# Strassen's scheme for the last four chunks of the MLP's first product in blocks 0 and 1

## The chip, the cores and the metric

One Trainium2 chip, one core of it. The metric is the device time of one execution in microseconds. Engines in the text: TensorE (PE), VectorE (DVE), ScalarE (ACT), GpSimd (POOL), SyncE (SP, which issues most DMAs).

## The reference

Two layers, each a linear attention and an MLP, on 2048 tokens of width 448, all in fp32:

```
x = x + attention(layernorm(x))        # 16 heads of 28, feature map elu(t)+1
x = x + gelu(layernorm(x) @ w1 + b1) @ w2 + b2     # w1: 448 x 1792, w2: 1792 x 448
```

The same weights serve both layers.

## The kernel before, in words

The tokens are cut into 16 tiles of 128, and these into four blocks of 512 (tiles 0 to 3 are block 0, and so on). The hidden width of 1792 is cut into 14 chunks of 128. A value that takes part in a matmul is split into a high part, which the matmul keeps exactly, and a low part (the rest); a product is three matmuls, high by high, low by high and high by low. ACT makes the high part by a cast (`XH`, `gh`), DVE or POOL the low part by a subtraction (`XL`, `gl`).

`mlp1` is the first product of one chunk of one block, the classic way: 11 matmuls 128x512 into the bank `hp` (L1205), then gelu on ACT and the split of g. The 448 rows of w1 are three pieces of 128 and one of 64; the last piece's low terms share matmuls, hence 11. `mlp2` is the second product of the chunk: for each of the block's four tiles three matmuls 128x448 into the bank `y` (L1235 to L1237). After the last chunk DVE adds `y` to the residual in `r` (L1240, called evacuation here) and SP stores it. Four banks hold `y`, so a new block's second product can begin only as the old block's four tiles are evacuated.

Blocks 0 and 1 go through all 14 chunks this way (`classic`). Blocks 2 and 3 go together, two chunks at a time, by Strassen's scheme (`eight(l, k)`, k from 0 to 6): the tokens of the two blocks are the rows and the pair's two chunks are the columns of a 2x2 matrix product, which takes seven products instead of eight. A11 and A12 are the two halves of block 2's width, A21 and A22 those of block 3; S1 = A21 + A22, S2 = S1 - A11, S3 = A11 - A21, S4 = A12 - S2. The seven products are 6, 5, 5, 5, 6, 6 and 6 matmuls 128x512, 39 where the classic way has 44. They add up in the banks `hx`, `hy`, `hz` (L1147): product 1 begins `hx`, ACT keeps a copy of it as `s1`, and product 6 goes on in the same bank; DVE adds the parts to `s1`, `s2` and `s5`. Two of the four results (block 2's) go on to gelu, split and `mlp2`; block 3's are stored as g in `g_d` and read back as `gb` in a last stage (`rest`), which does block 3's second product.

The sums S and the splits of all seven A and S (`token_sum`, L1112, by POOL for the first half of a tile and DVE for the second; `token_piece`, L1117 and L1118) are made while block 1 is at its last chunks. The tiles come as `sp`: DVE transposes 32x32 squares (`turn`), and a store to DRAM and a load back bring them into place (`store_sq`, `spread`). The weights' pieces are made by a generator per pair of chunks, `chunks` for a classic pair and `sevens` for a Strassen pair, advanced one step at a time by `make(n)`; two pairs fit into `W1` at once.

Every engine runs its instructions in the order in which the program writes them. What other work stands where among the chunks of blocks 0 and 1 is set by the table `PLAN`: one entry for each chunk, and each token of an entry is a piece of work (`behind`): q and p are steps of the attention's second half, o its output product, n the layernorm of a token tile, sx and lx store and load of its squares, sS.. a token sum, tA.. and tS.. a split, r and b the residual's reload and the bias. `ORDER` does the same for the stage ahead of the MLP.

Of the kernel before, what the change touches and what calls it, by code (L numbers as in the profile page):

```python
# [22 lines left out]
def linear_attn_mlp_kernel(  # L23
# [278 lines left out]
    squares, stored, spreads = {}, {}, {}  # L302
# [22 lines left out]
    def spread(key, h):  # L325
        d = stored.pop((key, h))
        if key[0] == "m" and (key[2], h) == (2, 1):
# [382 lines left out]
    def stage_g(l, t, acc, mid=lambda: None):  # L710
# [86 lines left out]
    def phase1(l, tr):  # L797
        za = consts.tile([128, D], F32, name="za", tag="za")
        acc = []
        load_to(l, 4 if l == 0 else NORM[l][1][-1])  # L800
        if l == 0:
            launch(za)
            load_to(l, NORM[l][2][-1])
        for t in range(l == 0, NT):
            norm = NORM[l][t] if t < len(NORM[l]) else ()
            for tok in STEPS.get((l, t), STEP).split():
                if tok[1:].isdigit() and tok[0] in "anv":
                    {"a": stage_a, "n": stage_n, "v": stage_t}[tok[0]](l, int(tok[1:]))
                elif tok == "q1":
                    stage_qphi(1)  # L810
                elif tok == "sp":
                    for key, h in list(stored):
                        block(key)
                        spread(key, h)
# [100 lines left out]
    def trans_chunks(tr):  # L915
# [4 lines left out]
        def rows(src, out, at, lo, hi):  # L920
            r = lo
            while r < hi:
                n = min(hi, (r // G + 1) * G) - r
                act.dma_start(f(out[at + r - lo:at + r - lo + n]), f(src[r // G][r % G:r % G + n]))
                r += n

        for c in range(3):
            for src, k in ((tr.Mh, 0), (tr.Ml, 1)):
                rows(src, tr.ch[c][k], 0, c * 128, (c + 1) * 128)
                yield  # L930
        rows(tr.Mh, tr.cr, 0, TL, D)
        rows(tr.Ml, tr.cr, 64, TL, D)
        yield


# [136 lines left out]
    def m_prep(l, b, j):  # L1072
# [5 lines left out]
              {"A11": 0, "S1": 5, "S2": 4, "A12": 1, "S3": 6, "S4": 2, "A22": 3})  # L1078
    SUMS = {"S1": ("A21", "A22", OP.add), "S2": ("S1", "A11", OP.subtract),
# [5 lines left out]
    def all_of(l, k, name):  # L1085

        at = PLACES[k][name]
        if at < 4:
            return (XH, XL)[k][:, at * 1024:][:, :1024]
        if (l, k, name) not in tall:  # L1090
            tall[l, k, name] = wide(k, at - 4, name)
        return tall[l, k, name]

    def placed(l, k, name, h):
        return all_of(l, k, name).rearrange("p (c h n) -> p h c n", c=2, h=2)[:, h]
# [28 lines left out]
    class Pair:  # L1124


        def __init__(self, l, p, n):
            self.l, self.p, self.n = l, p, n
            self.g = {}

        def product(self, k):
            at, name = PRODUCTS[k]
            w = W1[:, self.n % 2]
            hi, lo = (all_of(self.l, k, name) for k in range(2))
# [19 lines left out]
        def gelu(self, x, f):  # L1154
            g = t512("e", 5, "g")
            i = 2 * self.p + 1 - f
            for h in range(2):
# [12 lines left out]
        def later(self, x, f):  # L1170
            g = self.gelu(x, f)
            i = 2 * self.p + f
            g_d[self.l, i] = dram([128, 512], F32, f"g_d{self.l}_{i}")
            sp.dma_start(g_d[self.l, i], g)
# [35 lines left out]
    def mlp2(l, b, i, then=lambda: None):  # L1210
        gh, gl = gs.pop(i)
        first, last = i == 0, i == NF - 1
        n = i ^ (b > 1)
        hi, lo = w2h[:, n], w2l[:, n]
        end = l == LAYERS - 1 and b == NB - 1
        if first:
            accs[l, b] = [bank("acc", 4, f"y{j}")[:, :D] for j in range(4)]
        acc = accs[l, b]
        for j in range(4):
# [18 lines left out]
            if stop:  # L1238
# [4 lines left out]
                if last:  # L1243
                    sp.dma_start(x_d[l + 1][t * 128:(t + 1) * 128, :], xs)

    accs = {}
# [7 lines left out]
        "p10 z11",  # L1254
        "p11 sq10 z12 ld20",
        "p12 z13 lq10 ld21",
        "p13 sq11 z20 g10 ld22",
        "q10 lq11 p20 z21 g11 ld23",
        "q11 o10 p21 sq20 z22 g12",
        "q12 n10 o11 p22 z23 g13 ld30",  # L1260
        "q13 n11 o12 sx10 ld31",
        "n12 o13 lq20 p23 sq21 z30 ld32",
        "n13 lx10 sx11 p30 z31 g20 ld33",
        "lq21 p31 z32",
        "lx11 q20 x10 x11 sq30 g21",
        "q21 x12 x13 o20 p32 z33 g22",
        "q22 n20 o21 lq30 g23",
        "q23 n21 o22 p33 sq31 sx20 g30",
        "q30 n22 o23 g31",
        "q31 lq31 n23 o30 sx21 g32",  # L1270
        "q32 n30 o31 g33 r10 r11",
        "q33 n31 o32 sx30 lx21 r12 r13",
        "n32 o33 lx20 tA111 b10",
        "n33 sx31 lx30 tA121 b11",
        "lx31 tA110 b12",
        "sS10 sS11 tA120 b13",
        "tS10 tS11 sS30 sS20",
        "sS40 tS20 sS31 sS21",
        "tS21 sS41",
        "tS40 tS41",  # L1280
        "tS30 tS31",
    )

    def behind(l, i, tr):
        for tok in sorted(PLAN[i].split(), key=lambda tok: tok[0] != "l"):
# [27 lines left out]
            elif name == "x":  # L1313
                m_part(l, k, j)
            elif name == "r":
# [5 lines left out]
    ahead = [(l, "x" if b == 2 else "c", p) for l in range(LAYERS) for b in range(3) for p in range(NP)]  # L1321

    def first_pair(l, b):
        return (l * 3 + b) * NP

    def classic(l, b, tr):

        if b == 0:
            mlp1(l, 0, 0)
            moves = trans_chunks(tr)  # L1330
        for i in range(NF):
            if i + 1 < NF:
                mlp1(l, b, i + 1)
            elif b == 0:
                mlp1(l, 1, 0)
            if b == 0:
                next(moves, None)
            n = first_pair(l, b) + i // 2 + 2
            late = b and i >= NF - 4
            if late:  # L1340
                make(first_pair(l, 2))
            elif i % 2:
                make(n)
            if i % 2 == 0 and (b == 0 or i < NF - 2):
                make(n + 1)
            behind(l, b * NF + i, tr)
            if b == 0 and 5 <= i < 9:
                add_bias(l, 0, i - 5)
            if b == 0 or i < NF - 2:
                mlp2(l, b, i)  # L1350
            if b == 0:
                next(moves, None)
            if late:
                make(first_pair(l, 2))
            elif i % 2 == 0:
                make(n)

# [22 lines left out]
    def eight(l, k):  # L1380

        n = first_pair(l, 2) + k
        c = Pair(l, k, n)
# [40 lines left out]
        else:  # L1424
            step()
            mlp2(l, 1, NF - 2)
            c.product(2)
            dve.tensor_tensor(s1, s1, c.Z, op=OP.add)
            token_piece(l, "A22", 0)
            c.high(s1, 0)  # L1430
            make(n + 2)
            step()
            c.product(5)
            s5 = c.keep(c.Y, "s5")
            step()
            c.product(6)
            s2 = c.keep(c.X, "s2")
            c.low(0)
# [6 lines left out]
            make(n)  # L1445
            step()
            c.product(3)
            dve.tensor_tensor(s2, s2, c.Y, op=OP.add)
            c.high(s2, 1)
# [9 lines left out]
    class Came:  # L1459
# [6 lines left out]
        def load(self, l, n=1):  # L1466
            for i in range(self.n, min(self.n + n, NF)):
                tag = "EEFFeeee"[i % 8]
                self.x[i] = t512(tag, 5 if tag == "e" else 2, "gb")
                sp.dma_start(self.x[i], g_d[l, i])  # L1470
# [69 lines left out]
    for l in range(LAYERS):  # L1540
# [11 lines left out]
        def ahead_pq(j):  # L1552
# [15 lines left out]
            sa=lambda j: spread(("m", l, 0), j), pl=ahead_pq, z=lambda j: q_z(l, j, 0, tr), pre=lambda j: make(first_pair(l, 0) + 2), b=biases)  # L1568
# [5 lines left out]
        for b in range(2):  # L1574
            classic(l, b, tr)
        for k in range(NP):
# [30 lines left out]
```

## Time and profile before

| | |
|---|---|
| three runs | 850.35 us median (849.75 to 850.36) |
| the profiled execution | 850.62 us, its span 848.9 us |
| granted TensorE clock | 0.999 |
| busy in the span | PE 842.9 us, DVE 574.2, ACT 510.4, POOL 386.4 |
| matmul groups | `hp` 392 and 224 on high and low tokens (L1205), `y` 447 at each of L1235 to L1237 |
| DMA | 142.92 MB, mean 168 GB/s |

The span is what the profile shows of the execution; the 1.72 us beside it lie around it. Busy times of engines overlap. A group's busy time is a sum of durations as recorded; recorded matmuls overlap their neighbours.

### The profile page before, as it was taken

To read this page: it belongs to the slowest core of one execution; us is meant where nothing else is said; L and a number is where in the kernel's file an instruction comes from. 1 tells how busy PE (TensorE), PEld (TensorE's weight loads), DVE (VectorE), ACT (ScalarE), POOL (GpSimd) and SP (SyncE) were. 2 spreads that over 40 slices of the span, in tenths; PEclk is the share of its full clock that TensorE was granted. 3 is DMA by queue.
4 is the path that set the end of the run, shared out by engine and by line. 5 is a ranking of instruction groups with operands and counts; after the bars stand their busy time and mean duration, and the time that the engine had idled before them with its cause. 6 is when DMAs were issued, how large, how long until landed. Compare 5 with 4: busy or idle time off the path is not lost.

```text
span 848.9 us, 12473 instructions
## 1 busy us (share of the span) xinstructions
PE 842.9 (99%) x4085; PEld 754.8 (89%) x4085; DVE 574.2 (68%) x1022; ACT 510.4 (60%) x1051; POOL 386.4 (46%) x460
## 2 busy tenths in 40 slices
PE   9999999999999999999999999999999999999998
PEld 8899988888888888889999998988888888888897
DVE  7899597768733765556788976868686358544443
ACT  7667666475777567564446665555667766656521
POOL 3456534555426754650532343145742367454320
PEclk9999999999999999999999999999999999999999
DMA  5365847767667034437645543477666641333261
GB/s 166 123 241 183 254 121 220 244 208 239 209 199 240 14 125 132 135 112 239 217 152 175 172 142 120 135 226 246 215 203 229 224 161 34 114 94 103 89 236 44
DMA packets 103637, 142.92 MB, mean 168 GB/s; under 512 B 9876, under 2 KB 90644, under 8 KB 103572
## 3 DMA queue, kind: packets, MB, share of 16 engines
q1 hardware_dynamic: 101156, 138.77, 50.1%
q10 hardware_dynamic: 2416, 3.36, 1.3%
q8 instruction: 32, 0.52, 0.3%
q14 instruction: 33, 0.27, 0.1%
HBM read 88.94 MB, written 49.02 MB: 163 GB/s over the span
## 4 chain that ended last, share of the span: by engine, by line
PE 96%; DVE 2%; DMA 1%; POOL 1%; issue 0%; ACT 0%; SPq 0%; DVEq 0%; POOLq 0%; ACTq 0%
PE hp L1205 16%; PE y L1236 11%; PE y L1235 11%; PE y L1237 10%; PE hx L1147 9%; PE G L724 7%; PE psk L382 7%; PE psq L382 7%; PE hy L1147 4%; PE hz L1147 2%; PE op L1022 2%; PE op L1021 2%; PE op L1023 2%; PE op L1011 1%; PE op L1010 1%; PE op L1012 1%
## 5 line engine op out<-in xcount | busy, mean ns | idle before, releaser
L1236 PE MATMUL y<-w2l,gh 128*128 128x448 f32 x447 | 164.1, 367 | 0.0
L1235 PE MATMUL y<-w2h,gh 128*128 128x448 f32 x447 | 162.3, 363 | 0.0
L1237 PE MATMUL y<-w2h,gl 128*128 128x448 f32 x447 | 160.8, 360 | 0.0
L1182 DVE TENSOR_TENSOR gl<-g,gh 128x512 fp32r<-128x512 f32 x84 | 70.1, 835 | 103.1 <-ACT gh L1178 103.0
L1205 PE MATMUL hp<-XH,W 128*128 128x512 f32 x392 | 123.3, 389 | 0.0
L1235 PEld LDWEIGHTS y<-w2h,gh 128*128 128x128 f32 x447 | 83.8, 187 | 9.3
L1236 PEld LDWEIGHTS y<-w2l,gh 128*128 128x128 f32 x447 | 83.9, 188 | 6.8
L1237 PEld LDWEIGHTS y<-w2h,gl 128*128 128x128 f32 x447 | 84.0, 188 | 5.4
L1205 PE MATMUL hp<-XL,W 128*128 128x512 f32 x224 | 85.2, 389 | 0.0
L1205 PEld LDWEIGHTS hp<-XH,W 128*128 128x128 f32 x392 | 73.5, 188 | 12.6
L1207 ACT ACTIVATE g<-hp,b1s 128x512 f32<-128x512 f32 x56 | 38.5, 688 | 60.8 <-PE hp L1205 58.2
L1038 POOL TENSOR_TENSOR brs<-bst,few 128x1 f32<-128x1 f32 x32 | 18.7, 585 | 118.2 <-ACT bst L1036 116.8
L1159 ACT ACTIVATE g<-s,b1s 128x256 f32<-128x256 f32 x84 | 38.2, 502 | 55.5 <-DVE s L1413 34.9
L382 PE MATMUL psk<-wk,XH 128*128 128x448 f32 x210 | 61.8, 364 | 0.0
L563 POOL TENSOR_TENSOR xnl<-x,xnh 128x384 fp32r<-128x384 f32 x32 | 35.4, 1106 | 55.6 <-ACT xnh L562 27.8
L382 PE MATMUL psq<-wq,XH 128*128 128x448 f32 x196 | 57.2, 366 | 0.3 <-DVE eq L401 0.3
L1178 ACT CAST gh<-g 128x512 fp32r<-128x512 f32 x84 | 52.2, 622 | 2.7
L425 POOL TENSOR_TENSOR W<-temp,W 128x256 fp32r<-128x256 f32 x56 | 48.2, 880 | 7.5 <-ACT W L424 7.5
L1205 PEld LDWEIGHTS hp<-XL,W 128*128 128x128 f32 x224 | 42.0, 188 | 8.8
L213 POOL TENSOR_TENSOR brs<-bve,few 128x1 f32<-128x1 f32 x31 | 17.1, 551 | 66.9 <-DVE bve L212 61.5
L724 PE MATMUL G<-kh,xnh 128*128 128x448 f32 x128 | 46.6, 367 | 0.0
L724 PE MATMUL G<-kl,xnh 128*128 128x448 f32 x128 | 46.1, 366 | 0.0
(252 smaller groups left out, 2107.5 us busy)
## 6 DMA issues: line engine op xcount, KB each, us to landing
temp<-in_B_w_dram SPq DMA_DIRECT2D x28, 384.0 KB
x<-in_A_x_dram SPq DMA_DIRECT2D x32, 224.0 KB
pq_d<-eq SPq DMA_DIRECT2D x32, 224.0 KB
pq<-pq_d SPq DMA_DIRECT2D x32, 224.0 KB
g_d<-g SPq DMA_DIRECT2D x28, 256.0 KB
x<-x_d SPq DMA_DIRECT2D x32, 224.0 KB
gb<-g_d SPq DMA_DIRECT2D x28, 256.0 KB
sq_a<-sq SPq DMA_DIRECT2D x13, 512.0 KB
```

What stands on the lines that cost most here:

```text
L382: pe.matmul(o, x, p, start=(i == 0), stop=(i == 10))
L425: pool.tensor_tensor(lo, x, f(hi), op=OP.subtract)
L724: pe.matmul(acc[c], w, k, start=first and c not in others[0], stop=last and c not in others[1])
L1147: pe.matmul(o, w, r, start=(k in (1, 5, 2) and i == 0), stop=(i == len(made) - 1), skip_group_check=True)
L1159: act.activation(g[:, s].rearrange("p (u i n) -> p i u n", u=2, i=4), x[:, s].rearrange("p (i u n) -> p i u n", u=2, i=4), AF.Gelu_apprx_t ...
L1178: act.copy(gh, g)
L1182: dve.tensor_sub(gl, g, f(gh))
L1205: pe.matmul(hp, w, r, start=(k == 0), stop=(k == len(made) - 1))
L1207: act.activation(g, hp, AF.Gelu_apprx_tanh, bias=b1s[:, i:i + 1])
L1235: pe.matmul(acc[j], gh[:, s], hi, start=first, stop=False)
L1236: pe.matmul(acc[j], gh[:, s], lo, start=False, stop=False)
L1237: pe.matmul(acc[j], gl[:, s], hi, start=False, stop=stop)
```

## The change

`CUT = 10`: the classic way now does chunks 0 to 9 of blocks 0 and 1. The new `joint(l, k)`, k = 0 and 1, does chunks 10 to 13 of both blocks by the same seven products, block 1 as A11 and A12 and block 0 as A21 and A22, so that block 1's own split tiles serve as two of the seven (`FRONT`). Block 1's g goes straight to its second product. Block 0's is stored to `g_d`, its second product of chunks 0 to 9 is evacuated early and stored as a partial sum (`part_d`), and a later pass (`remainder` and the first pair `eight(l, 0)`) does chunks 11, 10, 13 and 12 with g and the sum read back. Block 0's unsplit tiles are kept in SBUF for the sums. `PLAN` is new, with two places in an entry (ahead of the "|" and behind it); the sums and splits of blocks 2 and 3 now stand in the remainder and in `eight(l, 0)`. The pairs of chunks 10 to 13 get their weights by `sevens`. Of the seven copies of the attention's combined weights `wq` two go through SP's queue before the MLP and the other five through ACT's, three to a chunk in place of two; q_scale and q_z of the first tile of block 1 stand ahead of the MLP.

```diff
+    FRONT = {"S1": 0, "A22": 1, "A11": 2, "A12": 3, "S3": 4, "S4": 5, "S2": 6}
...
+    def front_piece(l, name, h):
+        x = front_view(l, name, h)
+        hi, lo = (front(l, k, name, h) for k in range(2))
+        act.copy(hi, x)
+        dve.tensor_tensor(lo, x, f(hi), op=OP.subtract)
...
-        first, last = i == 0, i == NF - 1
+        part = int(b == 0 and i >= CUT)
+        first, last = (i == LATER[0], i == LATER[-1]) if part else (i == 0, i == (NF if b else CUT) - 1)
...
+    def load_part(l, t):
+        xt[l, t] = t448("H", 8, f"r{l}_{t}")
+        sp.dma_start(xt[l, t], part_d[l, t])
...
     PLAN = (
...
-        "lx31 tA110 b12",
-        "sS10 sS11 tA120 b13",
-        "tS10 tS11 sS30 sS20",
...
+        "sS11 tA120 tA121 tS10 sS30 sS20 tA111 sS31 c12",
+        "tS11 sS21 tS20 tS21 sS40 sS41",
...
+    CUT = 10
+    LATER = (11, 10, 13, 12)
...
+    def joint(l, k, tr):
...
+        c.product(1)
+        s1 = c.keep(c.X, "s1")
...
+            c.product(6)
+            s2 = c.keep(c.X, "s2")
+            c.low(0)
+            behind(l, 26, tr)
+            mlp2(l, 1, CUT - 1)
+            step()
+            c.product(7)
+            dve.tensor_tensor(s5, c.X, s5, op=OP.add)
+            c.later(s5, 1)
...
+    def remainder(l, tr):
+
+        mlp2(l, 1, NF - 1)
+        for k in range(2):
+            divide(LATER[k + 1], came.pop(LATER[k + 1]))
+            behind(l, 24 + k, tr)
+            mlp2(l, 0, LATER[k])
...
     def eight(l, k):
...
-            step()
-            mlp2(l, 1, NF - 2)
+            mlp2(l, 0, LATER[2])
+            behind(l, 27, None)
             c.product(2)
+            make(n + 2)
+            divide(LATER[3], came.pop(LATER[3]))
             dve.tensor_tensor(s1, s1, c.Z, op=OP.add)
-            token_piece(l, "A22", 0)
-            c.high(s1, 0)
...
             c.product(5)
             s5 = c.keep(c.Y, "s5")
             c.product(6)
             s2 = c.keep(c.X, "s2")
+            c.high(s1, 0)
             c.low(0)
-            mlp2(l, 1, NF - 1)
+            make(n)
+            mlp2(l, 0, LATER[3])
...
             c.product(7)
             dve.tensor_tensor(s5, c.X, s5, op=OP.add)
+            for h in range(2):
+                token_piece(l, "A22", h)
             c.later(s5, 1)
-            token_piece(l, "A22", 1)
```

Three places in the first layer show how instructions move; the rows are an engine's instructions in its order, equal neighbours counted with x. The first is DVE in the first pair of blocks 2 and 3, from the addition to s1 to the first split of weights after the evacuations; before, the low parts of A22 (`XL<-sp,A_3357`) are apart, and r_4 to r_7 are block 1's residual:

```order
L1428 TENSOR_TENSOR s_3333<-s_3333,hz 128x512
L1118 TENSOR_TENSOR XL<-sp,A_3357 128x2x256
L457 COPY raw<-W_130 128x256
L1182 TENSOR_TENSOR gl<-g,gh 128x512
L1240 TENSOR_TENSOR r_4_2877<-y_2659,r_4_2877 128x448
...
L1240 TENSOR_TENSOR r_7_2951<-y_2662,r_7_2951 128x448
L1442 TENSOR_TENSOR s_3379<-hx,s_3379 128x512
L1118 TENSOR_TENSOR XL<-sp,A_3357 128x2x256
L479 TENSOR_TENSOR W_130<-raw,W_130 64x128
L466 TENSOR_TENSOR W_130<-raw,W_130 128x512
```

The same place of the changed kernel, where r_0 to r_3 are block 0's residual and L1594 and L1607 are the additions to s1 and s5:

```order
L1594 TENSOR_TENSOR s_3408<-s_3408,hz 128x512
L1229 TENSOR_TENSOR gl<-g,gh 128x512
L486 TENSOR_TENSOR W_130<-raw,W_130 64x128
L1288 TENSOR_TENSOR r_0_3236<-y_3358,r_0_3236 128x448
...
L1288 TENSOR_TENSOR r_3_3242<-y_3361,r_3_3242 128x448
L464 COPY raw<-W_130 128x256
L1607 TENSOR_TENSOR s_3452<-hx,s_3452 128x512
L1162 TENSOR_TENSOR XL<-sp,A_3506 128x2x256 x2
L1613 TENSOR_TENSOR s_3460<-s_3460,hy 128x512
L473 TENSOR_TENSOR W_130<-raw,W_130 128x512
```

Both low parts of A22 now stand together behind gl, the evacuations, the copy and the addition to s5.

The second place is DVE's making of sums and splits of blocks 2 and 3. Before, in the last chunks of block 1 (S_3146 and the `sp` written by L1112 are sums):

```order
L1112 TENSOR_TENSOR S_3146<-sp 128x2x256
L1118 TENSOR_TENSOR XL<-sp,A_3067 128x2x256
L1182 TENSOR_TENSOR gl<-g,gh 128x512
L1118 TENSOR_TENSOR S_3189<-S_3146,XH 128x2x256 x2
L1182 TENSOR_TENSOR gl<-g,gh 128x512
L1118 TENSOR_TENSOR S_3234<-sp,S_3233 128x2x256
L1112 TENSOR_TENSOR sp<-sp 128x2x4x64
L1112 TENSOR_TENSOR sp<-S_3146,sp 128x2x4x64
L457 COPY raw<-W_130 128x256
L1182 TENSOR_TENSOR gl<-g,gh 128x512
```

Changed, in the remainder and the first pair (`gl<-gb,gh` are the low parts of block 0's chunks that came back; the last is chunk 12's):

```order
L1162 TENSOR_TENSOR XL<-sp,A_3345 128x2x256 x2
L1162 TENSOR_TENSOR S_3350<-S_3288,XH 128x2x256
L1162 TENSOR_TENSOR XL<-sp,XH 128x2x256
L1156 TENSOR_TENSOR sp<-sp 128x2x4x64
L1229 TENSOR_TENSOR gl<-gb,gh 128x512
L1162 TENSOR_TENSOR S_3350<-S_3288,XH 128x2x256
L1156 TENSOR_TENSOR sp<-S_3288,sp 128x2x4x64
L1162 TENSOR_TENSOR S_3382<-sp,S_3381 128x2x256 x2
L1156 TENSOR_TENSOR sp<-sp 128x2x4x64
L1162 TENSOR_TENSOR S_3422<-sp,XH 128x2x256 x2
L1162 TENSOR_TENSOR XL<-sp,XH 128x2x256 x2
L1229 TENSOR_TENSOR gl<-gb,gh 128x512
```

The work that was spread over block 1's last chunks, each with a classic first product, now stands in one piece. The third place is TensorE at the start of the four last chunks of the two blocks, first of before (block 1's last chunk 13, then block 2 and 3's first product):

```order
L1205 MATMUL hp<-XH,W_130 128x512
L1205 MATMUL hp<-XL,W_130 128x512
L1147 MATMUL hx<-XH,W_130 128x512 x2
L1147 MATMUL hx<-XL,W_130 128x512
L1147 MATMUL hx<-XH,W_130 128x512 x2
L1147 MATMUL hx<-XL,W_130 128x512
L1235 MATMUL y_2659<-w2h,gh 128x448
```

Changed, the first joint pair, whose product 1 follows the output product of the last token tile (`op`):

```order
L1041 MATMUL op<-wq_1678,qh 128x448
L1042 MATMUL op<-wq_1678,ql 128x448
L1191 MATMUL hx<-XH,W_130 128x512 x2
L1191 MATMUL hx<-XL,W_130 128x512
L1191 MATMUL hx<-XH,W_130 128x512 x2
L1191 MATMUL hx<-XL,W_130 128x512
L1283 MATMUL y_2370<-w2h,gh 128x448
```

Where a classic product stood before, products of Strassen's scheme now stand in blocks 0 and 1 too.

More of the change, by code (lines that the diff above doesn't have):

```diff
@@ L325, in spread @@
     def spread(key, h):
-        d = stored.pop((key, h))
-        if key[0] == "m" and (key[2], h) == (2, 1):
+        d = stored[key, h]
+        if key[0] == "m" and key[2] == 0:
+            l = key[1]
+            if (l, h // 2) not in kept:
+                kept[l, h // 2] = wide(h // 2, 2, "sp", F32)
+            r = kept[l, h // 2][:, h % 2 * 512:][:, :512]
+        elif key[0] == "m" and key[2] == 1:
+            r = wide(h, 1, "sp", F32)
+        elif key[0] == "m" and (key[2], h) == (2, 1):
             r = wide(0, 2, "sp", F32)
@@ L913, in trans_ms, with trans_chunks, rows @@
         dve.tensor_sub(tr.Ml[g], tr.mp[g], f(tr.Mh[g]))
-    def trans_chunks(tr):
+    def trans_chunks(tr, queues=(sp, sp, act, act, act, act, act)):
         tr.ch = [(piece("q", c), piece("q", 3 + c)) for c in range(3)]
         tr.cr = piece("q", 6)
-        def rows(src, out, at, lo, hi):
+        queue = iter(queues)
+        def rows(src, out, at, lo, hi, eng):
             r = lo
@@ L928, in trans_chunks, with trans_on @@
             for src, k in ((tr.Mh, 0), (tr.Ml, 1)):
-                rows(src, tr.ch[c][k], 0, c * 128, (c + 1) * 128)
+                rows(src, tr.ch[c][k], 0, c * 128, (c + 1) * 128, next(queue))
                 yield
-        rows(tr.Mh, tr.cr, 0, TL, D)
-        rows(tr.Ml, tr.cr, 64, TL, D)
+        eng = next(queue)
+        rows(tr.Mh, tr.cr, 0, TL, D, eng)
+        rows(tr.Ml, tr.cr, 64, TL, D, eng)
         yield
+    def trans_on(tr, n):
+        if not hasattr(tr, "moves"):
+            tr.moves = trans_chunks(tr)
+        for _ in range(n):
+            next(tr.moves, None)
     pqt, qs, pzs = {}, {}, {}
@@ L1133, in product @@
             w = W1[:, self.n % 2]
-            hi, lo = (all_of(self.l, k, name) for k in range(2))
+            hi, lo = (all_of(self.l, self.b, k, name) for k in range(2))
             u = [w[:, i * 128:(i + 1) * 128] for i in at]
@@ L1216, in mlp2 @@
         if first:
-            accs[l, b] = [bank("acc", 4, f"y{j}")[:, :D] for j in range(4)]
-        acc = accs[l, b]
+            accs[l, b, part] = [bank("acc", 4, f"y{j}")[:, :D] for j in range(4)]
+        acc = accs[l, b, part]
         for j in range(4):
@@ L1243, in mlp2, with behind @@
                 if last:
-                    sp.dma_start(x_d[l + 1][t * 128:(t + 1) * 128, :], xs)
-    accs = {}
-    PLAN = (
[L1254 to L1274, printed above, removed]
-        "lx31 tA110 b12",
-        "sS10 sS11 tA120 b13",
-        "tS10 tS11 sS30 sS20",
[L1278 to L1281, printed above, removed]
-    )
-    def behind(l, i, tr):
-        for tok in sorted(PLAN[i].split(), key=lambda tok: tok[0] != "l"):
+                    if b == 0 and not part:
+                        part_d[l, t] = dram([128, D], F32, f"part_d{l}_{t}")
+                    sp.dma_start(x_d[l + 1][t * 128:(t + 1) * 128, :] if b or part else part_d[l, t], xs)
+    accs, part_d = {}, {}
+    def load_part(l, t):
+        xt[l, t] = t448("H", 8, f"r{l}_{t}")
+        sp.dma_start(xt[l, t], part_d[l, t])
+    PLAN = (
[30 rows of a table added]
+    )
+    def behind(l, i, tr, part=0):
+        for tok in sorted((PLAN[i] + "|").split("|")[part].split(), key=lambda tok: tok[0] not in "lgc"):
             if tok[0] in "st" and tok[1] in "AS":
@@ L1326, in classic, with load_came @@
+    came = {}
+    def load_came(l, i):
+        tag = "EF"[len(came) % 2]
+        came[i] = t512(tag, 2, "gb")
+        sp.dma_start(came[i], g_d[l, 0, i])
     def classic(l, b, tr):
+        moves = iter(())
         if b == 0:
             mlp1(l, 0, 0)
-            moves = trans_chunks(tr)
-        for i in range(NF):
-            if i + 1 < NF:
+            turn(pqt.pop((l, 4)), ("q", l, 1), 0)
+            moves = tr.moves
+        then = first_pair(l, "j")
+        for i in range(CUT):
+            if i + 1 < CUT:
@@ L1333, in classic @@
                 mlp1(l, b, i + 1)
-            elif b == 0:
-                mlp1(l, 1, 0)
-            if b == 0:
+            for _ in range(2):
                 next(moves, None)
             n = first_pair(l, b) + i // 2 + 2
-            late = b and i >= NF - 4
+            late = b and i >= CUT - 4
             if late:
-                make(first_pair(l, 2))
+                make(then)
             elif i % 2:
                 make(n)
-            if i % 2 == 0 and (b == 0 or i < NF - 2):
+            if i % 2 == 0 and (b == 0 or i < CUT - 2):
@@ L1345, in classic @@
                 make(n + 1)
[L1346 to L1349, printed above, removed]
+            behind(l, b * CUT + i, tr)
+            if b == 0 and 1 <= i < 5:
+                add_bias(l, 0, i - 1)
+            if b == 0 and i == CUT - 1:
+                mlp1(l, 1, 0)
+            if b == 0 or i < CUT - 2:
                 mlp2(l, b, i)
-            if b == 0:
-                next(moves, None)
+            behind(l, b * CUT + i, tr, 1)
@@ L1353, in classic, with step @@
+            next(moves, None)
             if late:
-                make(first_pair(l, 2))
+                make(then)
             elif i % 2 == 0:
                 make(n)
+    def joint(l, k, tr):
+        n = first_pair(l, "j") + k
+        p = NC + k
+        c = Pair(l, 0, p, n)
+        def step():
+            make(n + 1)
+        c.product(1)
+        s1 = c.keep(c.X, "s1")
+        if k:
+            step()
+            c.product(5)
+            s5 = c.keep(c.Y, "s5")
+            step()
+            c.product(2)
+            dve.tensor_tensor(s1, s1, c.Z, op=OP.add)
+            c.high(s1, 0)
+            step()
+            c.product(6)
+            s2 = c.keep(c.X, "s2")
+            make(n)
+            make(n + 2)
+            step()
+            behind(l, 22, tr)
+            mlp2(l, 1, 2 * p - 1)
+            c.low(0)
+            step()
+            c.product(3)
+            dve.tensor_tensor(s2, s2, c.Y, op=OP.add)
+            c.high(s2, 1)
+            step()
+            c.product(7)
+            dve.tensor_tensor(s5, c.X, s5, op=OP.add)
+            c.low(1)
+            c.later(s5, 1)
+            step()
+            behind(l, 23, tr)
+        else:
+            behind(l, 20, tr)
+            step()
+            mlp2(l, 1, CUT - 2)
+            c.product(2)
+            dve.tensor_tensor(s1, s1, c.Z, op=OP.add)
+            c.high(s1, 0)
+            make(n + 2)
+            step()
+            c.product(5)
+            s5 = c.keep(c.Y, "s5")
+            step()
+            c.product(6)
+            s2 = c.keep(c.X, "s2")
+            c.low(0)
+            behind(l, 26, tr)
+            mlp2(l, 1, CUT - 1)
+            step()
+            c.product(7)
+            dve.tensor_tensor(s5, c.X, s5, op=OP.add)
+            c.later(s5, 1)
+            make(n)
+            step()
+            behind(l, 28, tr)
+            c.product(3)
+            dve.tensor_tensor(s2, s2, c.Y, op=OP.add)
+            c.high(s2, 1)
+            c.low(1)
+            step()
+            behind(l, 21, tr)
+        mlp2(l, 1, 2 * p)
+        if k:
+            divide(LATER[0], came.pop(LATER[0]))
+        c.product(4)
+        c.later(c.X, 0)
+        step()
+        if k == 0:
+            step()
@@ L1575, in linear_attn_mlp_kernel @@
             classic(l, b, tr)
+        for k in range(NP - NC):
+            joint(l, k, tr)
+        remainder(l, tr)
         for k in range(NP):
```

79 lines of the change are left out of this document (55 added, 24 removed), and 30 rows, old and new, of tables (ORDER, PLAN).

## The prediction

> **What bounds the kernel now.** I read the page first: the span, the busy shares, the granted clock and the engines of the chain that ended last.
>
> ```profile
> span 848.9 us, 12473 instructions
> PE 842.9 (99%) x4085; PEld 754.8 (89%) x4085; DVE 574.2 (68%) x1022; ACT 510.4 (60%) x1051; POOL 386.4 (46%) x460
> ...
> PEclk9999999999999999999999999999999999999999
> ...
> PE 96%; DVE 2%; DMA 1%; POOL 1%; issue 0%; ACT 0%; SPq 0%; DVEq 0%; POOLq 0%; ACTq 0%
> ```
>
> TensorE is busy for 99% of the span at full clock, and 96% of the chain is its own instructions. Then I asked what TensorE waits for.
>
> ```profile
> PE warm L171 <- DVE one L165: 1.1, 1, 1.1
> PE psk L652 <- ACT wk L138: 0.8, 1, 0.8
> PE psq L382 <- DVE eq L401: 0.3, 1, 0.3
> ```
>
> That is all: 2.2 us, none of it in the MLP. So the time is the number of matmuls times their spacing, and each microsecond that a new order makes TensorE wait is lost in full. The spacing I take from the chain in order of time, where pieces follow each other without a gap (start, length, what). The groups' means of nearly 0.4 us overlap and would overstate it.
>
> ```profile
> 141.72 2.49 PE hp L1205 x11
> 144.22 0.20 PE y L1235
> ...
> 293.11 1.36 PE hx L1147 x6
> ...
> 296.87 1.13 PE hz L1147 x5
> ```
>
> A 512-wide matmul costs 2.49 / 11 = 0.226 us in the classic first product and 1.36 / 6 = 1.13 / 5 = 0.227 us in Strassen's products; a 448-wide one costs 0.20.
>
> **Part 1, the matmuls.** In a layer four chunks of blocks 0 and 1 cost 4 x 2 x 11 = 88 matmuls by the classic way, and two joint pairs cost 2 x 39 = 78. That is 10 fewer in a layer, 20 in the program; the second product keeps its count. 20 x 0.227 = 4.54 us. The profiled execution took 850.62 us, 848.9 of span and 1.72 around it, 0.27 above the median of 850.35. With nothing lost it would come to 846.08, and the median to 845.8.
>
> **Part 2, the other engines' added work.** Per layer there are about 32 more DVE instructions, 8 ACT, 5 POOL and 20 DMA issues of SP: the sums and splits of blocks 0 and 1, a second evacuation of block 0, its partial sum and four chunks of g out and back. None is on the chain by its amount, since DVE is busy for 68% of the span. They cost only where TensorE arrives first. I went through the new order place by place, with prices from block 2's first pair (start, duration):
>
> ```profile
> 296.19 1.28 DVE L1118 TENSOR_TENSOR XL<-sp,XH 128x512 fp32r<-128x512 f32 x2
> 299.14 0.68 DVE L1428 TENSOR_TENSOR s<-s,hz 128x512 f32<-128x512 f32 x1
> 299.74 1.17 DVE L1118 TENSOR_TENSOR XL<-sp,A 128x512 fp32r<-128x512 f32 x1
> 300.83 0.83 DVE L457 COPY raw<-W 128x256 f32<-128x256 f32 x1
> 301.58 0.68 DVE L1182 TENSOR_TENSOR gl<-g,gh 128x512 fp32r<-128x512 f32 x1
> 302.18 2.21 DVE L1240 TENSOR_TENSOR r<-y,r 128x448 f32<-128x448 f32 x4
> ...
> 313.76 0.29 DVE L457 COPY raw<-W 128x256 f32<-128x256 f32 x1 [1.53 <-POOL W L430]
> 299.85 0.91 ACT L1159 ACTIVATE g<-s,b1s 128x256 f32<-128x256 f32 x2 [0.89 <-DVE s L1428]
> 300.79 0.62 ACT L1178 CAST gh<-g 128x512 fp32r<-128x512 f32 x1
> 297.35 0.57 ACT L1151 COPY s<-hx 128x512 f32<-128x512 f32 x1
> 299.62 0.74 POOL L430 TENSOR_TENSOR W<-raw,W 64x256 fp32r<-64x256 f32 x1
> 300.44 1.07 POOL L431 TENSOR_TENSOR W<-raw,W 128x256 fp32r<-128x256 f32 x1
> ```
>
> A 512-wide DVE operation on two SBUF tiles takes about 0.62 us alone (1.28 for two), and 1.17 beside POOL's operations at 299.62 and 300.44. The copy takes 0.29 alone and 0.83 beside POOL. Evacuations from PSUM take 0.55 each (2.21 / 4) with POOL at work, so they do not suffer.
>
> The Trainium skill, page "SBUF — State Buffer", section "SBUF: two separate sides", says that such a DVE operation and a GpSimd operation reading SBUF take one port pair as an exclusive lock, the loser blocked until the other ends. These rows agree: the piece that began 0.12 us after POOL's 0.74 us operation ended at 300.91, which is that operation's end (300.36) and a little under one free run.
>
> *Eight(0), product 4.* It reads the low parts of A22. In the changed DVE order they stand behind gl of s1, the four evacuations of block 0's later pass, the copy for W and the addition to s5. Count from the end of the second product of chunk 12. ACT starts gelu of s1 only after it has kept s2, that is after product 6, 2.40 us earlier (12 x 0.20). Keep, gelu and cast (0.57, 0.91, 0.62, with some 0.2 to start) and gl (0.68) end at about +0.6. A small split of W (0.3) and the evacuations (2.2) end at +3.1, the copy at +3.4, s5 at +4.0, the two pieces at +5.3. TensorE gets there after product 7, product 3 and chunk 0's second product, 1.36 + 1.13 + 2.40 = 4.89, and its third matmul, the first to read the low part, starts at 5.34. Alone everything fits to a hair. If the copy (+0.54) and both pieces (+0.55 each) run beside POOL, TensorE waits about 1.7 us. POOL's next four W operations are freed by that very copy, so some overlap is certain; I take 0.9, nearer the middle than either end because the pieces are shorter than POOL's row of work and one may slip past. By the skill's lock each could wait for a whole POOL operation of 1.07; that would make the place 2 x 1.07 + 0.54 = 2.7, and the sum 851.8, between the second rival below and the upper end.
>
> *The joint stage.* Product 6 of the first joint pair needs the low half of S2, which DVE makes among the last tokens' layernorm and transposes; product 6 of the second needs ACT to have kept s1, and ACT stands there in order behind a gelu that waits for DVE. Below nothing it cannot cost, as no wait was there to be removed. The upper ends are half a DVE operation beside POOL (1.17 / 2 = 0.6) for the first and one keep behind one split in a queue (0.57 + 0.62 = 1.2) if both add. I take 0.3, near the lower end: the chain of the fifteenth token is the only late one.
>
> *The remainder.* DVE has 18 operations on two SBUF tiles between the last evacuation of block 1 and the end of gl of chunk 12. Groups of before (busy, mean ns):
>
> ```profile
> L1182 DVE TENSOR_TENSOR gl<-gb,gh 128x512 fp32r<-128x512 f32 x28 | 22.7, 812 | 26.0 <-ACT gh L1178 25.4
> L1118 DVE TENSOR_TENSOR XL<-sp,A 128x512 fp32r<-128x512 f32 x8 | 7.5, 944 | 3.0 <-ACT A L1117 3.0
> L1112 DVE TENSOR_TENSOR sp<-sp 128x512 f32<-128x512 f32 x4 | 4.9, 1222 | 0.0
> L1118 DVE TENSOR_TENSOR S<-sp,S 128x512 fp32r<-128x512 f32 x4 | 4.5, 1115 | 0.3
> L1112 DVE TENSOR_TENSOR sp<-S,sp 128x512 f32<-128x512 f32 x2 | 3.3, 1671 | 0.1
> L1118 DVE TENSOR_TENSOR S<-sp,XH 128x512 fp32r<-128x512 f32 x4 | 2.6, 684 | 0.0
> L1112 POOL TENSOR_TENSOR sp<-sp 128x512 f32<-128x512 f32 x4 | 7.0, 1740 | 0.0
> ```
>
> TensorE does the second products of chunks 11, 10 and 13 and products 1, 2, 5 and 6 meanwhile: 3 x 2.40 + 3 x 1.36 + 1.13 = 12.4, and 0.4 more until a matmul reads gl. Evacuation ends some 0.75 after block 1's product, so DVE has about 12.0. Alone 18 x 0.61 = 11.0: hidden, with 1.0 to spare. At the groups' means, less the 0.08 by which neighbours overlap, it is about 16: late by 4.0. I take 0, because POOL's first sums (1.74 each and in the groups' contended state) can run in POOL's own queue before the evacuations and then touch few of the 18; the spare of 1.0 pays for two contended ones.
>
> *The turn from block 1's last second product to block 0's first later one* reuses the four banks at once. Before has the same turn at the start of block 3:
>
> ```profile
> 391.63 0.62 DVE L1240 TENSOR_TENSOR r<-y,r 128x448 f32<-128x448 f32 x1 [1.54 <-PE y L1237]
> ...
> 393.02 1.68 DVE L1240 TENSOR_TENSOR r<-y,r 128x448 f32<-128x448 f32 x3
> ```
>
> The chain has no wait of TensorE there, although a gl stood between the first and the other evacuations: nothing.
>
> *DMAs, and what moves.* The 20 more issues a layer stand on SP's queue; each value that returns is issued at least two second products (4.8 us) ahead of its use. Two of the seven copies of wq now go past SP and the others are issued earlier on ACT, and q_scale and q_z of block 1 run ahead of the MLP. ACT did wait on such copies before:
>
> ```profile
> 143.58 0.71 ACT L424 CAST W<-temp 128x256 fp32r<-128x256 f32 x2 [2.88 <-DMA wq<-Mh]
> 149.15 0.69 ACT L1207 ACTIVATE g<-hp,b1s 128x512 f32<-128x512 f32 x1 [2.33 <-DMA wq<-Ml]
> ```
>
> TensorE covered those (no wait in its list), and the first token that needs wq keeps some 2 us: nothing, at most 1 us a layer if that cover is gone.
>
> **The sum.** -4.54 + 2 x (0.9 + 0.3) = -2.1 us: 850.35 - 2.1 = 848.2 (the profiled one 848.5, span 846.8).
>
> **Rivals.**
> 1. *All is covered.* Every place fits at prices without POOL, as worked out: 845.8. For it: TensorE's list of waits before is empty in the MLP with much the same work beside it. Against it: product 4 has no spare at all.
> 2. *The waits eat the gain.* Both pieces and the copy beside POOL (1.7) and the joint stage at half its upper end (0.6) give 2.3 a layer, twice 4.6: about 850.4, no change. The point of balance is 4.54 / 2 = 2.27 a layer.
> 3. *The other side: DVE's backlog in the remainder.* If the 18 operations run at the groups' means, gl of chunk 12 is 4.0 late: -4.54 + 2 x 4.0 = +3.5, and 853.9, or with the forecast's 1.2 kept, 856.2. I say 855. It decides when more than 1.0 + 2.27 us of POOL's contention falls on DVE there, six operations of the 18 at 1.17 instead of 0.62.
>
> That the change does not do what it says is no rival: the order has the 20 matmuls fewer.
>
> **How the numbers follow.** Chances: the forecast 0.33 (its own range 846.6 to 849.6), all covered 0.27, gain eaten 0.22, backlog 0.18. The range leaves the backlog out: 845.5, a little under full cover, to 852.0, where 3.1 us a layer are lost. Within 0.2% (1.7 us, about what a measurement can tell from no change) is 848.65 to 852.05. Faster: full cover and two thirds of the forecast, 0.49. Same: the rest of the forecast and the eaten gain, 0.32. Slower: the backlog and a tail, 0.19.
>
> **What would show it.** In the profile of the changed kernel the first product's groups hold 20 matmuls fewer. TensorE's list of waits names A22's low part of DVE at product 4 with about 0.9 us, twice; the joint products' waits are under 0.5 each; none stands at the second products of chunks 13 and 12. If a wait on gl of chunk 12 of some microseconds is there, the third rival holds. If the list stays empty, the first does. The prediction is wrong if TensorE waits at a place not named here, such as for a partial sum or a square that comes back by DMA.

## The result and the profile after

The changed kernel takes 878.37 us (median; 877.32 to 880.1) beside 850.2 before: a ratio of 1.0334, interval 1.0321 to 1.0347. It is 28 us slower where 2 us less were forecast. The page of its profiled execution (878.53 us):

```profile
span 876.8 us, 12605 instructions
PE 852.7 (97%) x4065; PEld 754.6 (86%) x4065; DVE 616.4 (70%) x1086; ACT 520.4 (59%) x1075; POOL 406.1 (46%) x470
...
PE 47%; DVE 10%; DMA 7%; ACT 6%; issue 2%; SPq 1%; POOL 0%; DVEq 0%; ACTq 0%
...
L1252 PE MATMUL hp<-XH,W 128*128 128x512 f32 x280 | 88.4, 391 | 3.2 <-POOL W L438 1.7
```

The 20 matmuls are gone (4085 to 4065 records, `hp` on high tokens from 392 to 280). But the chain that ended last, 96% TensorE before, now runs through DVE, DMA and ACT too. TensorE's list of waits (total, times, longest) has grown from three rows to fifteen; those of the MLP of 0.4 us and more:

```profile
PE hy L1191 <- ACT op L1052: 4.0, 2, 2.0
PE y L1283 <- ACT gh L1225: 3.7, 2, 2.1
PE op L1038 <- ACT qh L371: 3.1, 2, 1.6
PE hp L1252 <- POOL W L438: 1.7, 2, 0.8
PE hp L1252 <- ACT XH L371: 1.5, 2, 0.8
PE op L1040 <- DVE ql L372: 1.4, 2, 1.0
...
PE y L1285 <- DVE gl L1229: 1.1, 2, 0.6
PE hx L1191 <- DVE XL L1162: 0.6, 2, 0.4
...
PE y L1283 <- DVE r L1288: 0.6, 2, 0.4
PE hy L1191 <- DVE S L1139: 0.4, 1, 0.4
```

These are 18.1 us. A second part is the granted clock, here in five stretches of 20 us (columns: the stretch, its length, busy time of PE, PEld, DVE, ACT and POOL, the granted clock with 1.00 for full speed, DMA share and GB/s):

```profile
150.00:170.00 20.00, 16.72 (x70) 13.92 (x69) 8.85 (x14) 11.14 (x24) 12.00 (x12) 0.91 0.65 213
260.00:280.00 20.00, 17.36 (x78) 13.84 (x76) 13.06 (x24) 13.96 (x31) 11.67 (x14) 1.00 0.40 131
580.00:600.00 20.00, 17.13 (x66) 14.11 (x65) 10.20 (x18) 9.36 (x20) 11.45 (x11) 0.83 0.64 213
690.00:710.00 20.00, 18.04 (x78) 15.22 (x77) 13.89 (x24) 13.95 (x31) 11.18 (x13) 0.91 0.44 140
730.00:750.00 20.00, 17.92 (x78) 15.23 (x77) 15.73 (x25) 11.63 (x24) 7.05 (x6) 0.91 0.39 137
```

(0.09 + 0.17 + 0.09 + 0.09) x 20 = 8.8 us of TensorE's cycles were not granted, always behind a wait. The whole account comes from the start times of all matmuls: start to start, less 0.200 us for a 448-wide and 0.227 for a 512-wide one. It holds waits and half clock together; the places are named by the time (us) at which they begin.

| place | layer 1 | layer 2 |
|---|---|---|
| start: block 1's first output products (from 150 and 580) | 5.7 | 6.7 |
| block 1's first chunk (195, 627) | 1.2 | 1.1 |
| joint stage (260, 690) | 3.9 | 3.9 |
| remainder and the turn ahead of it (296 to 313, 729 to 746) | 4.4 | 4.5 |
| product 4 of the first pair (321, 753) | 0.7 | 0.5 |

That is 32.6 us; less 4.5 for the matmuls it makes 28.1, and the span grew by 27.9. So the gain came as counted, and five places lost seven times as much. The table is of one execution: by the same count, the start cost between 4.2 and 7.7 us a layer in the profiles of experiments 1 to 8, which leave it as it is.

Two of them in layer 1. At the start, SP stores block 1's first squares and loads them back, and ACT needs them for qh, the high part of what the output product reads; ACT itself was held by its own issues of wq copies before that, but then stood idle for 2.5 us until the squares came:

```profile
144.54 0.32 SPq L323 DMA_DIRECT2D sq_q<-sq  x1
150.14 0.38 SPq L339 DMA_DIRECT2D sp<-sq_q  x1
...
151.35 0.62 ACT L436 CAST W<-temp 128x512 fp32r<-128x512 f32 x1 [4.46 <-DMA wq<-Ml]
155.69 1.14 ACT L371 CAST qh<-sp 128x512 fp32r<-128x512 f32 x2 [2.49 <-DMA sp<-sq_q]
156.36 0.47 PE L1038 MATMUL op<-wq,qh 128*128 128x448 f32 x1 [1.47 <-ACT qh L371]
```

The same in the kernel before:

```profile
149.38 0.32 SPq L323 DMA_DIRECT2D sq_q<-sq  x1
...
161.41 0.62 ACT L364 CAST qh<-sp 128x512 fp32r<-128x512 f32 x1 [1.13 <-DMA sp<-sq_q]
...
163.63 0.36 PE L1021 MATMUL op<-wq,qh 128*128 128x448 f32 x1
```

Store to cast took 12.0 us before and takes 11.2 now. But the output product stood four chunks behind the store in `PLAN` and now stands two and a half behind it. By the rows it began 14.3 us after the store before, without a wait; now TensorE has done its work ahead of it 10.2 us after the store (at 154.72) and can begin only at 11.8. In the remainder, chunk 13's g goes through DRAM:

```profile
293.87 0.72 ACT L1202 ACTIVATE g<-s,b1s 128x512 f32<-128x512 f32 x1
...
297.60 0.33 SPq L1221 DMA_DIRECT2D g_d<-g  x1
302.10 0.33 SPq L1399 DMA_DIRECT2D gb<-g_d  x1
...
305.18 0.62 ACT L1225 CAST gh<-gb 128x512 fp32r<-128x512 f32 x1 [5.73 <-DMA gb<-g_d]
```

SP reaches the store 3 us after g is there, behind four loads of the partial sum and two moves of W's pieces; the store takes 4.5, the load 3.0; ACT stands still for 5.7 us.

### The profile page after: what moved, and what is told of

Same layout as the page of the kernel before. It is cut to its first block, busy times and chain, and to the rows that moved or that the text cites. A ratio compares the mean times of both kernels' runs of the same rounds, so it can differ in the third digit from the quotient of the medians.

```text
span 876.8 us, 12605 instructions
## 1 busy us (share of the span) xinstructions
PE 852.7 (97%) x4065; PEld 754.6 (86%) x4065; DVE 616.4 (70%) x1086; ACT 520.4 (59%) x1075; POOL 406.1 (46%) x470
## 4 chain that ended last, share of the span: by engine, by line
PE 47%; DVE 10%; DMA 7%; ACT 6%; issue 2%; SPq 1%; POOL 0%; DVEq 0%; ACTq 0%
PE hx L1191 8%; PE y L1284 6%; PE y L1283 5%; PE y L1285 5%; PE G L731 4%; PE psk L389 4%; PE hy L1191 4%; PE psq L389 4%; PE hz L1191 2%; DMA sp<-sq_m 1%; PE hp L1252 1%; DMA g_d<-g 1%; DVE gl L1229 1%; DMA sq_m<-sq 1%; DVE ql L372 1%
## 5 line engine op out<-in xcount | busy, mean ns | idle before, releaser
L1229 DVE TENSOR_TENSOR gl<-g,gh 128x512 fp32r<-128x512 f32 x76 | 66.2, 871 | 50.8 <-ACT gh L1225 50.4
L1252 PE MATMUL hp<-XH,W 128*128 128x512 f32 x280 | 88.4, 391 | 3.2 <-POOL W L438 1.7
L1252 PEld LDWEIGHTS hp<-XH,W 128*128 128x128 f32 x280 | 52.4, 188 | 13.9 <-POOL W L438 2.5
L1252 PE MATMUL hp<-XL,W 128*128 128x512 f32 x160 | 60.6, 391 | 0.0
L968 POOL TENSOR_TENSOR pz<-pq,zb 128x448 f32<-128x448 f32 x26 | 31.8, 1221 | 50.6 <-DVE dn L979 29.5
L1225 ACT CAST gh<-gb 128x512 fp32r<-128x512 f32 x36 | 22.4, 621 | 52.9 <-PE y L1284 40.3
L1229 DVE TENSOR_TENSOR gl<-gb,gh 128x512 fp32r<-128x512 f32 x36 | 27.7, 770 | 31.6 <-ACT gh L1225 29.3
L1225 ACT CAST gh<-g 128x512 fp32r<-128x512 f32 x76 | 47.2, 621 | 2.4
L1076 POOL TENSOR_TENSOR r<-r,b2b 128x448 f32<-128x448 f32 x24 | 33.5, 1409 | 27.8 <-DMA r<-r_d 27.7
```

What stands on the lines that cost most here:

```text
L1076: pool.tensor_tensor(xt[l, t], xt[l, t], b2b, op=OP.add)
L1225: act.copy(gh, g)
L1229: dve.tensor_sub(gl, g, f(gh))
L1252: pe.matmul(hp, w, r, start=(k == 0), stop=(k == len(made) - 1))
```

## The experiments

All start from the changed kernel, each timed beside the kernel before. Their intervals reach 1.3 to 2.7 us to either side, so smaller differences between two versions can't be told from none. Waits are totals over both layers.

**1. g stays in SBUF.** Edit:

```diff
+            if self.b == 0:
+                came[i] = self.gelu(x, f, "EF"[i % 2])
+                return
...
-        sp.dma_start(came[i], g_d[l, 0, i])
```

> Block 0's g of chunks 10 to 13 stays in SBUF: gelu writes the tile that the load from DRAM filled, so 8 stores and 8 loads are gone and nothing else moves. Theory A (chains that end last set the time: the round trip of g through DRAM is one): TensorE's waits for gh in the remainder (3.7 us in all), for gl behind it (1.1) and the half clock that follows in layer 2 (about 2) go, about 6 to 7 us less: 871 to 873. Theory B (the added work of DVE and ACT is the bound there): the wait moves to gl or to the low parts of the sums, less than 2 us gained: 876 to 878.

879.77 us, ratio 1.034 (1.0321 to 1.036). The wait for gh is gone, and nothing is gained: 4.5 us of waits for `XL` at product 1 (and product 4) have come in its place, and those for gl are 2.0 in place of 1.1. The rows are of the slowest of its four executions (884.54; the others took 877.89 to 881.14). DVE and POOL there:

```profile
303.23 1.78 DVE L1162 TENSOR_TENSOR S<-S,XH 128x512 fp32r<-128x512 f32 x1
304.93 1.74 DVE L1162 TENSOR_TENSOR XL<-sp,XH 128x512 fp32r<-128x512 f32 x1
...
302.71 1.74 POOL L1156 TENSOR_TENSOR sp<-sp 128x512 f32<-128x512 f32 x1
304.53 1.59 POOL L1156 TENSOR_TENSOR sp<-S,sp 128x512 f32<-128x512 f32 x1
```

With ACT no longer standing still, DVE's splits meet POOL's sums, and each takes 1.75 us where the same two took 0.69 in the changed kernel. Theory B held in what it says of the wait, by a collision that the DRAM trip had hidden; the time is 2 us above its range.

**2. The loads of the partial sum later**, too (`y00` to `y03` from the middle of the joint stage into the remainder).

> As the run in which g stays in SBUF, and the four loads of the partial sum are issued later, in the remainder, so that SP issues the fold of W's pieces ahead of them; POOL stands in order behind that fold with the sums of blocks 2 and 3. Theory A (a queue in order holds the sums back until they meet DVE's): POOL's sums run before the evacuations, the waits for the low parts at product 1 (4.5 us) and for gl (2.0) go, 870 to 873. Theory B (DVE has simply too much there): the wait at product 1 stays above 1.5 us a layer, 877 or more.

876.65, ratio 1.0314 (1.0286 to 1.0343). The wait for `XL` is 5.0 us; that for gl is gone. A miss for theory A: POOL's sums moved 3.5 us ahead (from 302.71 to 299.25) and met other operations of DVE there, which took 1.78 and 1.75 us.

**3. Another bank for product 5.**

```diff
-                self.Y = bank("m", 2, "hy")
+                self.Y = bank("m" if self.b else "h", 2, "hy")
```

(and the second pair's `hx` from the op banks).

> In the joint stage product 5 accumulates in a bank of hp instead of the one that still holds the last token's op; the second joint pair's first product takes the op banks. Theory A: TensorE's wait for ACT's read of op (4.0 us in all) goes, but S2's low part comes only 3 us after product 6 wants it, so the wait moves to product 6: 876 to 878, with a new wait on S2 of about 2 to 3 us a layer. Rival: the bank alone held TensorE, 4 us and the half clock of layer 2 behind it (about 2) are gained: 872 to 873.

879.39, ratio 1.0345 (1.0329 to 1.036). The row for op is gone; in its place stands

```profile
PE hx L1191 <- ACT S L1138: 5.6, 2, 2.9
```

as theory A said, though the time is 1.4 us above its range: S2's split was the next chain, and no earlier.

**4. S2's splits ahead of the last token as well** (`f20 f21` in front of `o33`).

> As the run before, and the splits of S2 are written ahead of the last token's output product, so that ACT and DVE do them before that token's layernorm. Theory A: both waits go, 4.0 + 0.6 + 0.4 of waits and about 2 of half clock: 871 to 873. Rival (DVE is full there): the last token's chain is later by the two splits and its wait comes back at keeping s1 or at the sums: 876 to 878.

878.77, ratio 1.0344 (1.0316 to 1.0373). Now the third chain shows, ACT's keeping of s1 behind the last token's layernorm:

```profile
PE hx L1191 <- ACT s L1195: 5.8, 2, 3.1
```

The rival held, with the place that it named (its range missed by 0.8 us).

**5. That layernorm behind the keeping of s1.**

> As the run with another bank and S2 ahead, and of the last token only the output product stands ahead of the joint pair, its layernorm behind the keeping of s1. Theory A (ACT's order is the last of the three waits at this place): product 6 waits at most 0.7 us a layer, 5.8 us of waits and 3 of half clock gone, 869 to 873. Theory B (the place is bound by a chain whose ends follow each other closely): some wait of 1.5 us or more a layer is left at product 6 or behind it, 875 or more.

877.56, ratio 1.0331 (1.0299 to 1.0362). 3.9 us of waits stay, now at product 7 for the keeping of s2, and S4's low part follows with 1.1. Theory B.

**6. Experiments 2 and 5 together.**

> The first two of this call together. Theory A: the gains add, 862 to 867, with what is left at the start and at block 1's first chunk (about 14 us with their half clock). Theory B: 875 or more.

877.07, ratio 1.0321 (1.0291 to 1.035). Theory B: the two alone had won 1.7 and 0.8 us, less than the intervals tell, and together they win no more.

**7. Six repairs:** the same, with `tA111` first in the remainder and the last token's layernorm behind the keeping of s2.

> As the run of both repairs, and the split of A11's second half stands first in the remainder, and the last token's layernorm stands behind the keeping of s2. Theory A (each place has a few chains that end within some 3 us of each other, and these were the last two): joint stage and remainder keep under 1.5 us a layer, 864 to 868. Theory B (there are more behind them): 874 or more.

876.57, ratio 1.0306 (1.0286 to 1.0326). Waits for `XL` fell from 4.9 to 0.5 and for keeping from 3.9 to 0.5, S4's split waits 3.4, and gl 4.7, of which 4.0 in the remainder. Theory B. The reason for the last is two collisions again:

```profile
299.95 1.79 DVE L1162 TENSOR_TENSOR XL<-sp,XH 128x512 fp32r<-128x512 f32 x1
303.47 1.77 DVE L1162 TENSOR_TENSOR S<-S,XH 128x512 fp32r<-128x512 f32 x1
...
299.56 1.63 POOL L1156 TENSOR_TENSOR sp<-S,sp 128x512 f32<-128x512 f32 x1
303.09 1.60 POOL L1156 TENSOR_TENSOR sp<-sp 128x512 f32<-128x512 f32 x1 [1.90 <-DVE XL L1162]
```

POOL's end at 301.19 and 304.69, DVE's at 301.74 and 305.24: each 0.55 later, a little less than a free run takes (0.68).

**8. DVE makes POOL's sums too**, on top of the six.

```diff
-        eng = (pool, dve)[h]
+        eng = dve
```

> As the run of six repairs, but DVE makes POOL's halves of the four sums of blocks 2 and 3 too (four more operations on DVE in a layer, none of POOL in that stretch). Theory A (a DVE operation on two SBUF tiles stands still while POOL's runs): the three long ones in the remainder (0.81, 1.79 and 1.77 us in six repairs) come to 0.69, 2.3 us less, against three more operations of 0.61 ahead of gl of chunk 13: the wait for gl in the remainder stays within 0.7 of its 2.2 us a layer, and the time within 2 us of six repairs. Theory B (the long ones have another cause): they stay, and the wait for gl grows by 1.8 a layer, 878 or more.

872.6, ratio 1.027 (1.0253 to 1.0288): DVE got four more operations a layer, and the kernel became 4 us faster where theory A expected no more than 2 us of difference. The same two operations of DVE:

```profile
299.53 0.68 DVE L1162 TENSOR_TENSOR XL<-sp,XH 128x512 fp32r<-128x512 f32 x1
...
301.94 0.68 DVE L1162 TENSOR_TENSOR S<-S,XH 128x512 fp32r<-128x512 f32 x1
```

and the waits for gl in the remainder fell from 4.0 to 2.2. So the collisions are shown as a cause of these waits, by taking POOL's operations away. They are not all of the 4 us: by the start times of the matmuls the remainder and product 4 lost 2.0 us less than in experiment 7, and block 1's first chunk in layer 2, which the edit leaves alone, 1.5 less. This is the best version found; it is still 22 us behind the kernel before.

**9. All copies of wq by SP** (`queues=(sp,) * 7`).

> All seven copies of wq are issued by SP, none by ACT. Theory A (the start is a token's chain through DRAM that is too long): TensorE's wait for POOL's W (1.7) goes because ACT is no longer held by its issues, the waits for qh and ql (4.5) and the half clock stay: 876 to 877. Rival (the copies of wq cause the whole delay at the start, by holding ACT): all of 6 us and 4 of clock go: 867 to 870. Second rival: SP issues later what the tokens need, 880 or more.

884.13, ratio 1.0397 (1.0382 to 1.0413). The wait for W is gone, as theory A said, but

```profile
PE op L1038 <- ACT qh L371: 10.7, 2, 5.5
```

instead of 3.1: what SP issues for the tokens now stands behind the copies (in layer 1 the store at 145.40, the load at 152.92, the cast at 158.62). ACT has no copies to issue and stands idle for 8.3 us until the squares are there. The second rival held.

**10. The output product half a chunk later**, and what follows it.

> The first token's output product of block 1 stands half a chunk later in the table, and what follows it in the same chunks with it. Theory A (block 1's token chain has 10 chunks instead of 14 to run in and is longer than these): the wait for qh and ql (4.5 us) goes, but TensorE only arrives earlier at the first chunk of block 1, where the wait for XH grows from 1.5 to about 5; 876 to 879. Rival (the token stood too early, no more): 869 to 872.

884.9, ratio 1.0421 (1.0399 to 1.0443). The waits at the output product fell from 4.5 to 1.4 us, but others took their place:

```profile
PE y L1285 <- DVE gl L1229: 7.3, 4, 2.7
PE y L1283 <- ACT gh L1225: 4.6, 4, 1.5
```

Not at block 1's XH, as theory A had it (that row is gone), but for the most part in the chunks ahead of it (2.7 us for gl at 190.04 and again at 624.75), where the later steps hold DVE and ACT; and it was 6 us slower than no repair. That the delay moves on instead of going is shown; theory A's place and size were wrong.

**11. Idle work in the waits:** 33 matmuls a layer, overwritten, ahead of four of the waits.

> The changed kernel with idle TensorE work ahead of four of its waits in each layer: 12 matmuls of 448 ahead of block 1's first output product, 4 ahead of its first chunk, 9 of 512 ahead of product 2 of the first joint pair and 8 ahead of product 1 of the first pair of blocks 2 and 3. They are overwritten; together 7 us of TensorE a layer, 14 in all. Theory A (other engines' chains set the end of these places, and the half clock after a wait costs time of its own): the waits are filled, the clock stays up, 870 to 873. Theory B (the chains set the end, and the half clock hides under the next wait): 877 to 880. Rival (TensorE is still the bound): 14 more, 892.

877.04, ratio 1.0326 (1.0296 to 1.0356). 14 us more of TensorE cost nothing. The same five stretches:

```profile
150.00:170.00 20.00, 18.53 (x89) 16.01 (x87) 9.64 (x16) 11.96 (x27) 11.50 (x12) 1.00 0.69 227
260.00:280.00 20.00, 19.33 (x86) 15.53 (x85) 13.05 (x25) 13.08 (x29) 12.70 (x14) 1.00 0.39 129
580.00:600.00 20.00, 19.02 (x92) 16.80 (x91) 9.09 (x16) 11.33 (x25) 11.66 (x12) 1.00 0.66 224
690.00:710.00 20.00, 19.21 (x85) 15.35 (x85) 13.05 (x23) 13.88 (x31) 11.77 (x14) 1.00 0.40 129
730.00:750.00 20.00, 19.11 (x87) 15.63 (x86) 15.48 (x26) 10.20 (x21) 9.11 (x9) 1.00 0.44 152
```

The clock stays up, 8.8 us of cycles are back, and the time falls by 1.3 us, which is within the interval. Theory B: other engines' chains set the end of these places, and most of the half clock hides under the next of them. Whether all of it does, these runs can't tell: the changed kernel's six executions lie between 877.32 (granted clock 0.996) and 880.1 (0.988), while the four here, all at 0.999, still differ by 5.5 us.

**12. Idle work in every classic chunk:** 9 matmuls more in each.

> The changed kernel with 9 more matmuls of 512, overwritten, in each of the 20 classic chunks of a layer: 2.04 us a chunk, 81.7 us in all. Theory A (the start and block 1's first chunk lack cover: tokens' chains have 10 chunks where they had 14): the 14 us of waits and half clock there go, those of the joint stage, the remainder and product 4 (18 us) stay, as their cause is the order next to them: 878 + 82 - 14 = 946. Rival (DVE has too much work in the whole MLP stage): all waits go, 929. Second rival (PE-bound): 960.

941.7, ratio 1.1077 (1.1061 to 1.1094): 63 us more for 82 of TensorE. All waits at the start, at block 1's first chunk and for op are gone; in layer 1 the output product now begins 15.1 us after the store (148.44 to 163.52), about as far as before. Apart from the warm-up's row only these stay above 1 us:

```profile
PE y L1287 <- DVE gl L1229: 2.4, 3, 1.5
PE y L1285 <- ACT gh L1225: 1.7, 1, 1.7
PE hx L1191 <- DVE XL L1162: 1.6, 3, 1.0
```

all in the stages that got no idle work. Between theory A (946) and the first rival (929), nearer to A: the classic stage lacks time for the chains beside it, and the joint stage lost its wait for op along with that. That 63 us of the 82 show in the time also says that TensorE is still the bound over most of a chunk.

## Why the prediction was wrong

- **The matmuls** were right: 20 fewer, 4.5 us in the account.
- **"nothing, at most 1 us a layer if that cover is gone", on DMAs and what moves,** is the step that failed, by the most: the start and block 1's first chunk cost 6.9 us in layer 1 and 7.8 in layer 2. I had taken 2 us of reserve over from the old order. But the tokens of block 1 now had 10 chunks instead of 14, and their way through DRAM keeps its 11 us: the 14.3 us from store to output product had become 10.2. A wait for a square that comes back by DMA was the prediction's own sign of being wrong. I looked for the cost where instructions were added (Strassen's sums) and not where time was taken away: each chunk that leaves a stage takes 4.9 us of cover (2.49 + 12 x 0.20) from everything that runs beside it. Experiment 12 shows it, where the distance given back ends the wait, and experiment 9, where a longer way through DRAM lengthens it though ACT is free; experiment 10 shows that the steps behind have no room either.
- **"Each value that returns is issued at least two second products ahead"** counted from the load. The load itself waits for the store, the store for SP's queue: 11.3 us from gelu to cast, 3.7 us of waits in the remainder. Experiment 1 takes these away, and the next chain is as late.
- **The joint stage** was put at 0.3 a layer and cost 3.9. I had S2's split and the keeping of s1, the second and the third chain, and had priced them at 0.6 and 1.2 at most; the bank that op holds I missed. Experiments 3 to 5 bring them out one behind the other.
- **The remainder's backlog** was the third rival, and it was there, but covered by ACT's stop; it came out in experiments 1 and 7, at product 1 and at gl of chunk 13 and not at gl of chunk 12.
- **The price of DVE beside POOL** was too low. I read 1.17 from a row where POOL's operation took 0.74 us. It is what is left of POOL's operation and then 0.55; beside POOL's sums 1.75 to 1.79. The Trainium skill's page "SBUF — State Buffer", section "SBUF: two separate sides", has it as an exclusive lock for the whole instruction; these rows agree to the hundredth, and its sentence should have set the price. At product 4, where the prediction did try it, the 2.7 us did not come: the two pieces together cost 0.55 more than alone, and the copy nothing (0.28 at 319.21).
- **Product 4** was the one place forecast with a cause that held: 0.9 a layer forecast, 0.7 and 0.5 measured, A22's two pieces taking 1.83 us in place of 1.28.

```profile
320.01 1.83 DVE L1162 TENSOR_TENSOR XL<-sp,A 128x512 fp32r<-128x512 f32 x2
```

- **The turn** of the four banks was put at nothing and waited 0.6 us in all.
- The forecast and its rivals had one thing in common that the runs refute: they priced each wait alone, on a kernel bound by TensorE. At four places of each layer TensorE is no longer the bound, as 14 us of idle work there at no cost show. Then a wait that is taken away leaves the next chain, which is about as late: for op 4.0 us, then 5.6 for S2, 5.8 for s1 and 3.9 for s2 (experiments 3 to 5).

Still open: which chains would be left at the start after a repair there, and what holds the joint stage and the remainder after six repairs, where they still cost 6.3 and 7.0 us over both layers by the count of the table. No version with an earlier start of block 1's tokens was run, so whether the scheme can pay in these two blocks isn't settled.

## What to carry to other kernels

When a change takes work off the bounding engine, list what ran beside that work and ask of each chain, from its first store to its last cast, whether it still fits; the average load of the other engines says nothing of it. Test it cheaply by giving the bounding engine idle work at its waits: if that costs no time, the bound has already moved there, and repairing one wait may only show the next. Count a round trip through DRAM from the producer's end, with the issuing queue's other work in it. Price a DVE operation on two SBUF tiles beside POOL by what is left of POOL's operation, which can be the whole of it, and then a free run.

## What the runs showed of the hardware

The clock was not expected to matter. In layer 2 it fell to half behind a single wait of 2.1 us at 697.6 (from the last matmul's start at 697.59 to the next at 699.93, less one spacing of 0.227; columns as above):

```profile
698.00:700.00 2.00, 0.07 (x1) 0.07 (x1) 1.46 (x4) 1.05 (x4) 0.16 (x1) 1.00 0.58 216
700.00:702.00 2.00, 2.00 (x6) 1.50 (x7) 0.77 (x2) 2.00 (x5) 0.98 (x2) 0.66 0.88 249
702.00:704.00 2.00, 2.00 (x6) 1.57 (x6) 1.42 (x3) 1.05 (x3) 1.55 (x2) 0.50 0.81 257
```

while behind the same wait of layer 1, 265.22 to 267.60, it stayed at 1.00 (the stretch 260 to 280 above). The Trainium skill's page "TensorE: Matmul & The Clock Gate", section "HAM oscillation — how this bites in real kernels", puts the limit at gaps of about 3.4 us; here a gap of 2.1 us was enough once and not the other time, so for this kernel the measured rows decide.
